# An attention and gated MLP block on one core: denominators' reciprocals spread by two DMAs through HBM in place of a VectorE transposition, with a changed planner

## The chip, the cores and the metric

The kernel runs on one core of one Trainium2 chip. Its time is the device time in microseconds (us); lower is better. Before the change it takes 1222.69 us, the median of 3 runs (1222.42 to 1225.06).

The engines are TensorE (PE, with its weight loads shown as PEld), VectorE (DVE), ScalarE (ACT), GpSimd (POOL) and SyncE (SP). Each runs its own list of instructions in a fixed order and waits on semaphores of the others. The core's 16 DMA engines move data; an engine's queue issues the transfers (SPq is SyncE's).

## What is computed

All inputs and the output are bf16. In short (`x` is 2048 x 512, 32 heads, 2048 cached keys and values a head, 128 wide; the MLP is 1792 wide):

```python
xn = _layernorm(x)
q = (xn @ wq).reshape(B, Sq, H, Dh)            # per head: 2048 x 128
p = softmax(q @ k_cache.T * Dh ** -0.5)        # per head: 2048 x 2048
s = (p @ v_cache).reshape(Sq, H * Dh) @ wo
r = relu(xn @ w1 + b1)
g = silu((r * r) @ w2 + b2)
out = x + s * g
```

## The kernel before

**Blocks, heads and pairs.** The 2048 rows are cut into NQB = 4 blocks of QB = 512. A block runs through 32 heads, so there are NG = 128 units, called heads below and numbered g. A head's 2048 keys are 16 tiles of 128, taken two at a time: NPR = 8 steps a head, NPAIR = 1024 steps in all (loop at L1421).

**One step.** `gen_scores` (L670) multiplies two key tiles with the queries into PSUM (psA), transposed, so that keys lie on partitions; ScalarE takes the exponential of 128 x 1024 values into one of NPT = 8 buffers pT. Two steps later `gen_pv` (L964) multiplies by V. Between them come one or two matmuls of filler work from a list of jobs: the query projection of later heads (`job_proj`), the MLP (`job_h`, `job_o2`) and the output projection (`job_wo`).

**Two kinds of heads.** In the first kind pT is stationary and V, widened by a column of ones, streams: 64 matmuls of 129 columns a head. The denominator falls out as the 129th column, one value a row on its own partition; VectorE copies the sum out (o_un), takes the reciprocal, GpSimd scales, and a transposing DMA turns the result into oT. In the second kind (V stationary, `gen_pv_b`, L725) 16 matmuls of 512 columns give the output already transposed; ScalarE copies it to o_col (NOC = 3 buffers). The denominator must then be summed over keys, which lie on partitions, and be spread over all 128 partitions along the row. Heads 0 to 2 and the last 3 are of the first kind; for the others `choose` (called at L1425) takes the second kind when VectorE's debt `owed` (L960) is under OWED = 9000 ns. m counts the heads of the second kind; buffers of the denominators' chain alternate by m % 2.

**The denominators' chain before.** For each pT buffer either VectorE sums it alone in one transposing reduction (`den_part`, L744), or GpSimd first adds its halves (`part_add`, L757, into h_sum) and VectorE reduces 512 columns (`part_half`, L765). `den_sum` (L776) adds the eight steps to d_sum, 128 x 16, in which every group of 32 partitions holds a partial sum. `den_write` and `den_read` (L783, L790) are two DMAs on SyncE: to d_scr in HBM, and back with all four groups on every partition. `den_total` (L798) adds the four, `den_recip` (L804) inverts, and `den_spread` (L809) is a transposition on VectorE of 32 x 32 blocks of a broadcast, which writes r_all, 128 x 512 f32, one buffer. `den_scale` (L817) on GpSimd multiplies o_col by r_all into oT.

**What sets the order.** The program emits every engine's list ahead of time with a model of each engine's clock (`_cost`; `_ISSUE` at L97 gives a DMA's issue and landing times). Small VectorE work waits in the list `quiet` with a due step and is placed by `fill_dve` (L904) where VectorE has room; `fill_pool` (L921) and `fill_sync` (L948) do the same for GpSimd and SyncE as soon as the model says that an operand is there. `ready_at` (L890) adds SLACK = 1500 ns to what depends on a DMA (den_total, den_read). `fill_pool` takes a `part_add` whenever GpSimd is free and one of three h_sum buffers is. On the chip the order is fixed; a wait stops what stands behind it.

**Loads.** SyncE also issues all keys (two transposing DMAs a head, `fill_k`, L628), values (four a head, `fill_v`, L640) and query weights, two to three heads ahead, and between steps 2 and 150 the MLP's and output weights.

**LayerNorm.** Each block's four tiles of 128 rows are loaded to x_ln (`ln_load`, L474), normalised (`ln_bn`, `ln_rstd`, `ln_scale`) to xn_t and transposed by DMA (`ln_next`, L517). x_ln and xn_t have four tiles each.

Helper lines in the profile: L226 and L231 matmuls (the second for the first kind of heads and the first head), L235 activations, L239 tensor-tensor, L245 and L249 tensor-scalar forms, L253 copies, L257 reciprocals, L282 reductions, L286 transposing reductions, L290 the transposition, L294 DMAs, L298 transposing DMAs.

Of the kernel before, what the change touches and what calls it, by code (L numbers as in the profile page):

```python
# [84 lines left out]
def _uses_port(name, fn):  # L85
# [3 lines left out]
    if name == "DVE":  # L89
        if f in (_tt, _stt):  # L90
            return _in_sbuf(k["in0"]) and _in_sbuf(k["in1"])
        if f in (_ts, _copy):
# [6 lines left out]
          "d_quad": (1230, 4200)}  # L99
# [201 lines left out]
def bass_recurrent_scan__mha_block_cached__dense_activation_squared_relu__prompt_kernel(  # L301
# [41 lines left out]
    OWED = 9000  # L343
# [16 lines left out]
    NSL, NSW, NQS, NPT, NOT, NOC, NHS = 3, 4, 3, 8, 3 * HC, 3, 3  # L360
# [20 lines left out]
    d_sum = sb("d_sum", [P, 2, NBK], F32)  # L381
    d_quad = sb("d_quad", [P, 2, 4, NBK], F32)
    d_rec = sb("d_rec", [P, 2, NBK], F32)
    r_all = sb("r_all", [P, NBK, 32], F32)
    d_scr = nc.dram_tensor("d_scr", [2, 32, 4 * NBK], F32, kind="Internal").ap()
# [6 lines left out]
    x_ln = sb("x_ln", [P, TPB, D], BF16)  # L392
    xn_t = sb("xn_t", [P, TPB, D], BF16)
    st_t = sb("st_t", [P, TPB, 12], F32)
    mv_t = sb("mv_t", [P, TPB, 2], F32)
    nm_t = sb("nm_t", [P, TPB], F32)
# [3 lines left out]
    warm = sb("warm", [P, P], BF16)  # L400
# [33 lines left out]
    sl_dr = [S.slot(f"dr{i}") for i in range(2)]  # L434

# [22 lines left out]
    t_ones = None  # L458
    for i in range(NSL):
        t_ones = E(GP, partial(_memset, out=v_sb[:, i, :, Dh:Dh + 1], val=1.0))  # L460
# [12 lines left out]

    def ln_load(j, i, eng=SP):  # L474
        jt = j * TPB + i
        t_xl[jt] = S.emit_dma(
            eng, partial(_dma, out=x_ln[:, i, :], in_=A_x[0, jt * P:(jt + 1) * P, :]), sl_xl[i],
            deps=[t_xn.get(jt - TPB)])
# [3 lines left out]
    def ln_bn(j, i, c0=0, c1=D):  # L482
        jt = j * TPB + i
        k = 6 if c0 else 0
        t_bn[jt] = E(DV, partial(_bn_stats, out=st_t[:, i, k:k + 6], in_=x_ln[:, i, c0:c1]),
                     deps=[t_xl[jt], t_xn.get(jt - TPB), t_xr.get(jt - TPB)])
# [15 lines left out]
    def ln_scale(j, i):  # L502
        jt = j * TPB + i
        t_xn[jt] = E(DV, partial(_ts, out=xn_t[:, i, :], in0=x_ln[:, i, :],
                                 scalar1=mv_t[:, i, 0:1], scalar2=rstd[:, i:i + 1],
                                 op0=ALU.subtract, op1=ALU.mult),
                     deps=[t_xr[jt], t_xnr.get(jt - TPB)])

    def ln_transpose(j, i):
        jt = j * TPB + i  # L510
        t_xnr[jt] = tok_xT[j][i] = S.emit_dma(
            SP, partial(_dmaT, out=xnT[:, :, jt % (2 * TPB) * P:(jt % (2 * TPB) + 1) * P],
                        in_=xn_t[:, i, :]),
            sl_xT[i], deps=[t_xn[jt], t_xuse.get(j - 2)])
        assert j < 2 or n_xuse[j - 2] == NFC + H

    def ln_next(j, i):  # L517
        ln_scale(j, i)
        ln_transpose(j, i)

# [38 lines left out]
    def first_transpose(i):  # L559
        for c in range(NDC):  # L560
            t_xT[i] = E(PE, partial(_peT, out=bankF(1)[:, 0:256].bitcast(BF16)[:, c * P:(c + 1) * P],
                                    in_=xn_t[:, i, c * P:(c + 1) * P], ident=ident[:]),
                        deps=[t_xn[i], t_ident, tok_xT[0][i - 1] if i else None],
                        inc=(c == NDC - 1))
        t_xnr[i] = t_xT[i]
# [147 lines left out]
    t_sum = {}  # L713
    t_dw = {}
    t_dr = {}
# [60 lines left out]
    def den_sum(g):  # L776
        m = b_no[g]
        t_sum[m] = E(DV, partial(_reduce, out=d_sum[:, m % 2, :],
                                 in_=d_part[:, m % 2, 0:len(t_parts[g]), :].rearrange(
                                     "p n b -> p b n")),  # L780
                     deps=t_parts[g] + [t_dw[m - 2] if m >= 2 else None])

    def den_write(g):  # L783
        m = b_no[g]
        dst = bass.AP(tensor=d_scr.tensor, offset=d_scr.offset + m % 2 * P * NBK,
                      ap=[[NBK, 4], [4 * NBK, 32], [1, NBK]])
        t_dw[m] = S.emit_dma(SP, partial(_dma, out=dst, in_=d_sum[:, m % 2, :]), sl_dw[m % 2],
                             deps=[t_sum[m], t_dr[m - 2] if m >= 2 else None])

    def den_read(g):  # L790
        m = b_no[g]
        src = bass.AP(tensor=d_scr.tensor, offset=d_scr.offset + m % 2 * P * NBK,
                      ap=[[0, 4], [4 * NBK, 32], [1, 4 * NBK]])
        t_dr[m] = S.emit_dma(SP, partial(_dma, out=d_quad[:, m % 2].rearrange("p a b -> p (a b)"),
                                         in_=src), sl_dr[m % 2],
                             deps=[t_dw[m], t_tot[m - 2] if m >= 2 else None])

    def den_total(g):  # L798
        m = b_no[g]
        t_tot[m] = E(DV, partial(_reduce, out=d_rec[:, m % 2, :],  # L800
                                 in_=d_quad[:, m % 2].rearrange("p a b -> p b a")),
                     deps=[t_dr[m], t_spr.get(m - 2)])

    def den_recip(g):  # L804
        m = b_no[g]
        t_rec[m] = E(DV, partial(_recip, out=d_rec[:, m % 2, :], in_=d_rec[:, m % 2, :]),
                     deps=[t_tot[m]])

    def den_spread(g):  # L809
        m = b_no[g]  # L810
        base = d_rec[:, m % 2, :]
        spread = bass.AP(tensor=base.tensor, offset=base.offset,
                         ap=[list(base.ap[0]), [1, NBK], [0, 32]])
        t_spr[m] = E(DV, partial(_transpose32, out=r_all[:], in_=spread),
                     deps=[t_rec[m], t_scale[m - 1] if m else None])

    def den_scale(g):  # L817
        m = b_no[g]
        t_scale[m] = tok_oT[g] = E(
            GP, partial(_tt, out=oT[:, g % NOT, :], in0=o_col[:, m % NOC, :],  # L820
                        in1=r_all[:].rearrange("p b i -> p (b i)"), op=ALU.mult),
            deps=[t_col[m], t_spr[m], t_wodone[g - NOT] if g >= NOT else None])
# [5 lines left out]
    tiles = {}  # L828
    WEIGHT = {den_part: 1130, part_half: 610, den_sum: 350, den_total: 170, den_recip: 130,
              den_spread: 600}  # L830
# [4 lines left out]
    def plan_b(g):  # L835
        tiles[g] = 0
        first = NPR * g
        for k in range(NPR):
            calm(first + k + NPT - 2, partial(den_part, NPR * g + k))
        calm(first + NPR + 6, partial(den_sum, g))  # L840
        sync_quiet.append(partial(den_write, g))
        sync_quiet.append(partial(den_read, g))
        calm(first + NPR + 12, partial(den_total, g))
        calm(first + NPR + 12, partial(den_recip, g))
        calm(first + NPR + 13, partial(den_spread, g))
        pool_quiet.append(partial(den_scale, g))

    def needs(fn):
# [6 lines left out]
        if f in (den_sum, den_total, den_recip, den_spread, den_scale, den_write, den_read):  # L855
            g = a[0]
            m = b_no[g]
            if f is den_sum:
                if tiles[g] < NPR:
                    return None  # L860
                return t_parts[g] + [t_dw.get(m - 2) if m >= 2 else t_parts[g][0]]
            if f is den_write:
                return [t_sum.get(m), t_dr.get(m - 2) if m >= 2 else t_sum.get(m)]
            if f is den_read:
                return [t_dw.get(m), t_tot.get(m - 2) if m >= 2 else t_dw.get(m)]
            if f is den_total:
                return [t_dr.get(m), t_spr.get(m - 2) if m >= 2 else t_dr.get(m)]
            if f is den_recip:
                return [t_tot.get(m)]
            if f is den_spread:  # L870
                return [t_rec.get(m), t_scale.get(m - 1) if m else t_rec.get(m)]
            return [t_col.get(m), t_spr.get(m)]
# [17 lines left out]
    def ready_at(fn):  # L890
        toks = needs(fn)
        if toks is None or any(t is None for t in toks):
            return None
        slack = SLACK if fn.func in (den_total, den_read) else 0
        return S.ready(toks) + slack
# [25 lines left out]
    def fill_pool(until):  # L921
        while GP.t < until:
# [6 lines left out]
            if x < NHS or t_half[x - NHS] is not None:  # L929
# [127 lines left out]
    def at(step, fn):  # L1057
        events.setdefault(step, []).append(fn)
# [141 lines left out]
    def load_xt(jt):  # L1200
        if jt < NQB * TPB:
            tok_xt[jt] = S.emit_dma(
                GP, partial(_dma, out=x_t[:, jt % 2, :], in_=A_x[0, jt * P:(jt + 1) * P, :]),
                sl_xt[jt % 2], deps=[t_u[jt - 2] if jt >= 2 else None])
# [142 lines left out]
    for j in range(NQB):  # L1347
        if j + 1 < NQB:
            for i in range(TPB):
                at(j * SPB + 3 * NPR, partial(ln_load, j + 1, i))  # L1350
# [59 lines left out]
    t_bankF[:] = [t_q0[3], tok_xT[0][3]]  # L1410
    gen_pv(3)
# [9 lines left out]
    for pi in range(NPAIR):  # L1421
        g, k = divmod(pi, NPR)
        if k == 0 and g > 0:
            m = len(b_heads)
            choose(g, FIRST_B <= g < NG - 3 and owed(pi) < OWED and (m < NOC or m - NOC in t_dr))  # L1425
            if is_b(g):
                plan_b(g)
# [78 lines left out]
```

## Time and profile before

| | before |
|---|---|
| median of 3 runs | 1222.69 us |
| profiled execution | 1225.06 us, span 1223.3 us |
| granted TensorE clock | 1.00 |
| PE busy | 1207.6 us (99% of the span) |
| DVE, ACT, POOL busy | 1083.0, 1090.1, 1074.9 us (89, 89, 88%) |
| DMA | 174.80 MB, 143 GB/s; SyncE's queue 69.0% of the 16 engines' span |
| heads with V stationary | 113 (count of o_col and of r_all) |
| r_all on VectorE (L290) | 113 x 680 ns, 76.8 us |
| oT on GpSimd (L239) | 113 x 1274 ns, 143.9 us |
| h_sum on GpSimd (L239) | 772 x 1166 ns, 876.3 us |
| d_part from h_sum, from pT (L286) | 772 x 685 ns, 132 x 1210 ns |

The profile is of one execution. Busy times are sums of an engine's instructions without the waits; matmuls are pipelined, so two that follow each other overlap in the rows, and the distance between their starts is the time each one costs. A few matmul records are missing from a trace. An idle engine costs nothing unless TensorE, or what TensorE waits for, stands behind it.

### The profile page before, as it was taken

Reading aid. Unit: us, or ns where it says so; the run is one execution under the profiler, and the core shown is the slowest. Engines: PE = TensorE matmul, PEld = TensorE weight load, DVE = VectorE, ACT = ScalarE, POOL = GpSimd, SP = SyncE. Lnnn points to the kernel's source line nnn. Section 1 sums busy time; section 2 is a strip of 40 time slices with the busy share of each in tenths; the row PEclk is TensorE's granted clock in tenths of the full one; section 3 lists DMA queues with packets and bytes.
Section 4 is the critical chain, followed back from the end, with each engine's and each line's share of the span. In section 5 each row is a group of like instructions: output and inputs, shape, how many; then the busy total and the mean of one; then the engine's idle time right before and its main releaser. Section 6 shows DMA issues by size and latency. Waiting matters only on the chain.

```text
span 1223.3 us, 19712 instructions
## 1 busy us (share of the span) xinstructions
PE 1207.6 (99%) x6339; PEld 585.9 (48%) x6461; DVE 1083.0 (89%) x1829; ACT 1090.1 (89%) x1158; POOL 1074.9 (88%) x986
## 2 busy tenths in 40 slices
PE   9999999999999999999999999999999999999998
PEld 7544444444545444444544445444445454444555
DVE  4689989999998999989899998889999999999973
ACT  7888999999898999999998998999999989989995
POOL 1788999999897999999888998999998979999881
PEclk9999999999999999999999999999999999999999
DMA  9998978667777666666777666667667666667661
GB/s 199 190 210 170 188 158 157 133 132 137 143 152 148 133 135 134 135 136 127 149 143 159 133 135 146 133 131 141 132 138 149 138 143 138 131 129 134 130 137 32
DMA packets 665567, 174.80 MB, mean 143 GB/s; under 512 B 652248, under 2 KB 664280, under 8 KB 665464
## 3 DMA queue, kind: packets, MB, share of 16 engines
q1 hardware_dynamic: 663368, 169.47, 69.0%
q0 software_dynamic: 1424, 3.81, 1.2%
q8 instruction: 51, 0.84, 0.3%
q14 instruction: 52, 0.43, 0.1%
q10 hardware_dynamic: 672, 0.26, 0.1%
HBM read 100.31 MB, written 3.02 MB: 84 GB/s over the span
## 4 chain that ended last, share of the span: by engine, by line
PE 92%; DVE 3%; POOL 2%; issue 1%; DMA 1%; ACT 0%; ACTq 0%; SPq 0%; POOLq 0%
PE psA L226 34%; PE psO L226 30%; PE psF L226 24%; PE psO L231 4%; POOL h_sum L239 1%; DVE d_part L286 1%; DMA d_quad<-d_scr 0%; ACT pT L235 0%; DVE h2T L249 0%; POOL oT L239 0%; DVE acc L249 0%; DVE r_t L245 0%; PE psA L231 0%; DMA d_scr<-d_sum 0%; DMA x_ln<-in_A_x_dram 0%
## 5 line engine op out<-in xcount | busy, mean ns | idle before, releaser
L235 ACT ACTIVATE pT<-psA 128x1024 bf16<-128x1024 f32 x1025 | 1037.7, 1025 | 114.0 <-PE psA L226 74.2
L239 POOL TENSOR_TENSOR h_sum<-pT 128x512 f32<-128x512 bf16 x772 | 876.3, 1166 | 43.6 <-DVE d_part L286 23.5
L226 PE MATMUL psA<-qt_sb,kT 128*128 128x512 bf16 x1972 | 591.5, 379 | 5.0 <-ACT pT L235 2.3
L286 DVE TRANSPOSE_TENSOR_REDUCE d_part<-h_sum 128x16 f32<-128x512 f32 x772 | 512.7, 685 | 32.5 <-POOL h_sum L239 29.7
L226 PE MATMUL psO<-pT,v_sb 128*128 128x512 bf16 x1771 | 529.7, 379 | 2.6 <-DVE o_un L253 0.5
L226 PEld LDWEIGHTS psA<-qt_sb,kT 128*128 128x128 bf16 x2032 | 193.6, 98 | 216.4 <-ACT pT L235 5.5
L226 PEld LDWEIGHTS psO<-pT,v_sb 128*128 128x128 bf16 x1808 | 176.7, 98 | 213.9 <-issue 2.3
L226 PE MATMUL psF<-xnT,wq_sb 128*128 128x512 bf16 (+1 forms) x510 | 165.9, 374 | 2.4 <-DVE h2T L249 1.2
L239 POOL TENSOR_TENSOR oT<-o_col,r_all 128x512 bf16<-128x512 f32 x113 | 143.9, 1274 | 23.1 <-DVE r_all L290 22.4
L286 DVE TRANSPOSE_TENSOR_REDUCE d_part<-pT 128x32 f32<-128x1024 bf16 x132 | 158.9, 1210 | 3.5 <-ACT pT L235 3.3
L226 PE MATMUL psF<-wo_all,oT 128*128 128x512 bf16 x471 | 161.2, 379 | 0.7
L253 DVE CAST qt_sb<-psF 128x512 bf16<-128x512 f32 (+1 forms) x130 | 86.6, 666 | 24.6 <-PE psF L226 22.5
L226 PEld LDWEIGHTS psF<-xnT,wq_sb 128*128 128x128 bf16 x520 | 50.2, 98 | 62.4 <-issue 3.1
L290 DVE STREAM_TRANSPOSE r_all<-d_rec 128x512 f32<-128x512 f32 x113 | 76.8, 680 | 0.4
L226 PE MATMUL psF<-xnT,w_sb 128*128 128x512 bf16 x221 | 76.2, 379 | 0.5 <-DVE h2T L249 0.2
L231 PEld LDWEIGHTS psO<-v_sb,pT 128*128 128x128 bf16 x960 | 63.8, 98 | 26.8 <-ACT pT L235 0.4
L226 PEld LDWEIGHTS psF<-wo_all,oT 128*128 128x128 bf16 x480 | 46.9, 98 | 56.4
L231 PE MATMUL psO<-v_sb,pT 128*128 128x129 bf16 x960 | 73.7, 220 | 0.1
L226 PE MATMUL psF<-w_sb,h2T 128*128 128x512 bf16 x221 | 72.7, 379 | 0.4
L235 ACT ACTIVATE o_col<-psO 128x512 f32<-128x512 f32 x113 | 66.8, 591 | 0.0
L245 DVE TENSOR_SCALAR r_t<-psF,b1f 128x512 bf16<-128x512 f32 x56 | 41.2, 736 | 12.3 <-PE psF L226 11.0
L282 DVE TENSOR_REDUCE d_sum<-d_part 128x16 f32<-128x144 f32 (+3 forms) x113 | 43.2, 382 | 1.0
(61 smaller groups left out, 407.4 us busy)
## 6 DMA issues: line engine op xcount, KB each, us to landing
v_sb<-in_A_v_cache_dram SPq DMA_DIRECT2D x508, 128.0 KB, 2.6
wq_sb<-in_A_wq_dram SPq DMA_DIRECT2D x127, 128.0 KB, 2.7
wo_all<-in_A_wo_dram SPq DMA_DIRECT2D x16, 256.0 KB, 3.1
kT<-in_A_k_cache_dram SPq DMA_TRANSPOSE x254, 3.4
d_quad<-d_scr SPq DMA_DIRECT2D x113, 32.0 KB
w_sb<-in_B_w_dram SPq DMA_DIRECT2D x14, 256.0 KB, 3.6
x_t<-in_A_x_dram POOLq DMA_DIRECT2D x16, 128.0 KB, 3.0
x_ln<-in_A_x_dram SPq DMA_DIRECT2D x15, 128.0 KB, 2.7
```

The source lines that it names most:

```text
L226: return e.matmul(out, lhsT, rhs, start=start, stop=stop)
L231: return e.matmul(out, lhsT, rhs, start=start, stop=stop, skip_group_check=True)
L235: return e.activation(out, in_, func, bias=bias, scale=scale)
L239: return e.tensor_tensor(out, in0, in1, op)
L245: return e.tensor_scalar(out, in0, scalar1=scalar1, scalar2=scalar2, op0=op0, op1=op1)
L253: return e.tensor_copy(out, in_)
L282: return e.tensor_reduce(out, in_, axis=AX.X, op=ALU.add)
L286: return e.tensor_reduce(out, in_, axis=AX.X, op=ALU.add, apply_transpose=True)
L290: return e.transpose(out, in_)
```

## The change

- The reciprocals are no longer spread by VectorE. `den_turn`, a VectorE transposition of 128 x 32, puts d_sum's blocks into rows before the write, `den_read` brings the four partial sums to 32 partitions only, `den_total` and `den_recip` work on these 32, and two new DMAs on SyncE, `rec_write` and `rec_read`, write the 512 reciprocals to r_scr in HBM and read them back onto all 128 partitions. r_all has two buffers; o_col has four (NOC = 4).
- The planner: OWED is 8000; GpSimd takes a part_add only while VectorE's debt is over POOL_OWED = 3500; SLACK also stands before rec_read and den_scale; part_half gets HALF_SLACK = 600.
- Space: x_ln and xn_t have two tiles each; block 0's tiles 2 and 3 use x_t and out_t, later blocks load tiles 2 and 3 after tiles 0 and 1 are scaled. The warm-up operand lies in o_bf.
- The change's title names 116 heads with V stationary. The number and size of the load pieces (NKP, NVP, NWP) are the same in both kernels.

The diff, cut to its core:

```diff
-          "d_quad": (1230, 4200)}
+          "d_quad": (530, 4200), "r_scr": (530, 2200), "r_all": (1230, 4400)}
...
-    OWED = 9000
+    OWED = 8000
+    POOL_OWED = 3500
+    HALF_SLACK = 600
...
-    NSL, NSW, NQS, NPT, NOT, NOC, NHS = 3, 4, 3, 8, 3 * HC, 3, 3
+    NSL, NSW, NQS, NPT, NOT, NOC, NHS = 3, 4, 3, 8, 3 * HC, 4, 3
...
-    r_all = sb("r_all", [P, NBK, 32], F32)
-    d_scr = nc.dram_tensor("d_scr", [2, 32, 4 * NBK], F32, kind="Internal").ap()
+    r_all = sb("r_all", [P, 2, QB], F32)
+    d_scr = nc.dram_tensor("d_scr", [2, P, 32], F32, kind="Internal").ap()
+    r_scr = nc.dram_tensor("r_scr", [2, QB], F32, kind="Internal").ap()
...
+    t_sum0 = E(GP, partial(_memset, out=d_sum[:], val=0.0))
...
     def ln_next(j, i):
         ln_scale(j, i)
         ln_transpose(j, i)
+        if i + 2 < TPB:
+            ln_load(j, i + 2)
...
+    def den_turn(g):
+        m = b_no[g]
+        t_row[m] = E(DV, partial(_transpose32, out=d_row[:, m % 2, :], in_=d_sum[:, m % 2, :]),
+                     deps=[t_sum[m], t_dw.get(m - 2)])
...
-        dst = bass.AP(tensor=d_scr.tensor, offset=d_scr.offset + m % 2 * P * NBK,
-                      ap=[[NBK, 4], [4 * NBK, 32], [1, NBK]])
-        t_dw[m] = S.emit_dma(SP, partial(_dma, out=dst, in_=d_sum[:, m % 2, :]), sl_dw[m % 2],
-                             deps=[t_sum[m], t_dr[m - 2] if m >= 2 else None])
+        t_dw[m] = S.emit_dma(SP, partial(_dma, out=d_scr[m % 2], in_=d_row[:, m % 2, :]),
+                             sl_dw[m % 2], deps=[t_row[m], t_dr.get(m - 2)])
...
-                      ap=[[0, 4], [4 * NBK, 32], [1, 4 * NBK]])
+        src = bass.AP(tensor=d_scr.tensor, offset=d_scr.offset + m % 2 * P * 32,
+                      ap=[[NBK, 32], [32 * 32, 4], [1, NBK]])
+        t_dr[m] = S.emit_dma(SP, partial(_dma, out=d_quad[0:32, m % 2], in_=src), sl_dr[m % 2],
+                             deps=[t_dw[m], t_tot.get(m - 2)])
...
-    def den_spread(g):
+    def rec_write(g):
         m = b_no[g]
-        base = d_rec[:, m % 2, :]
-        spread = bass.AP(tensor=base.tensor, offset=base.offset,
-                         ap=[list(base.ap[0]), [1, NBK], [0, 32]])
-        t_spr[m] = E(DV, partial(_transpose32, out=r_all[:], in_=spread),
-                     deps=[t_rec[m], t_scale[m - 1] if m else None])
+        t_rw[m] = S.emit_dma(
+            SP, partial(_dma, out=r_scr[m % 2].rearrange("(p b) -> p b", b=NBK),
+                        in_=d_rec[0:32, m % 2, :]),
+            sl_rw[m % 2], deps=[t_rec[m], t_spr.get(m - 2)])
+
+    def rec_read(g):
+        m = b_no[g]
+        src = bass.AP(tensor=r_scr.tensor, offset=r_scr.offset + m % 2 * QB,
+                      ap=[[0, P], [1, QB]])
+        t_spr[m] = S.emit_dma(SP, partial(_dma, out=r_all[:, m % 2, :], in_=src), sl_rr[m % 2],
+                              deps=[t_rw[m], t_scale.get(m - 2)])
...
-        slack = SLACK if fn.func in (den_total, den_read) else 0
+        slack = SLACK if fn.func in (den_total, den_read, rec_read, den_scale) else (
+            HALF_SLACK if fn.func is part_half else 0)
...
-            if x < NHS or t_half[x - NHS] is not None:
+            if (x < NHS or t_half[x - NHS] is not None) and owed(now[0]) > POOL_OWED:
...
-                at(j * SPB + 3 * NPR, partial(ln_load, j + 1, i))
+                if i < 2:
+                    at(j * SPB + 3 * NPR, partial(ln_load, j + 1, i))
```

## The prediction

> **What bounds the kernel now.** I read the page's busy line first, then the busy time by stretches, then the chain of waits, then the timeline around the places where TensorE stood still. The busy line and four stretches (columns: start:end, length, then busy time of PE, PEld, DVE, ACT, POOL with the instruction counts, the granted clock, the DMA engines' share, GB/s):
>
> ```profile
> PE 1207.6 (99%) x6339; PEld 585.9 (48%) x6461; DVE 1083.0 (89%) x1829; ACT 1090.1 (89%) x1158; POOL 1074.9 (88%) x986
> ```
> ```profile
> 50.00:110.00 60.00, 55.24 (x295) 26.23 (x300) 53.64 (x91) 48.92 (x53) 49.80 (x48) 1.00 0.91 189
> 110.00:300.00 190.00, 189.05 (x864) 86.12 (x881) 172.77 (x294) 173.55 (x186) 185.26 (x167) 1.00 0.76 154
> 300.00:320.00 20.00, 19.35 (x137) 10.64 (x137) 18.79 (x31) 16.75 (x18) 17.18 (x17) 1.00 0.86 144
> 320.00:660.00 340.00, 338.21 (x1685) 160.10 (x1718) 312.23 (x527) 309.13 (x328) 310.45 (x283) 1.00 0.69 140
> ```
>
> TensorE is the bound, at full granted clock, and it is nearly gapless. From 110 to 300 us it lacks 0.95 of 190 us (0.5%), from 320 to 660 us 1.79 of 340 us (0.5%); the same 0.5% everywhere is what some missing matmul records would leave, so I count it as no idle time. Above that 0.5% only two places are left: 50 to 110 us, 60 - 55.24 = 4.8 us less 0.3, so 4.4 us; and 300 to 320 us, 0.65 less 0.1, so 0.5 us. The first 50 us lack 1.6 us in the start-up, which the change leaves as it is. So **at most 4.9 us can be won from idle time**, almost all of it in one early stage.
>
> What that stage waits for (timeline: start, length, engine, what it does, then the idle time before it and who ended it):
>
> ```profile
> 54.72 3.04 SPq L298 DMA_TRANSPOSE kT<-in_A_k_cache_dram  x1
> 57.81 0.69 SPq L294 DMA_DIRECT2D d_scr<-d_sum  x1
> 58.55 0.98 SPq L294 DMA_DIRECT2D v_sb<-in_A_v_cache_dram  x2
> 60.77 0.57 SPq L294 DMA_DIRECT2D d_quad<-d_scr  x1
> ```
> ```profile
> 63.14 0.26 DVE L282 TENSOR_REDUCE d_rec<-d_quad 128x16 f32<-128x64 f32 x1 [3.91 <-DMA d_quad<-d_scr]
> ```
> ```profile
> 64.16 1.15 POOL L239 TENSOR_TENSOR h_sum<-pT 128x512 f32<-128x512 bf16 x1 [4.58 <-DVE d_rec L257]
> ```
> ```profile
> 100.88 3.65 DVE L245 TENSOR_SCALAR xn_t<-x_ln,mv_t,rstd 128x512 bf16<-128x512 bf16 x1
> ```
>
> SyncE's queue is late (a transposing load took 3.04 us to issue), the denominators' round trip through HBM lands late, VectorE stands 3.91 us in its fixed order, GpSimd 4.58 us behind it, and TensorE pays when the next evacuations come late. At 100.88 us a scaling that takes 0.37 us at its quickest takes 3.65 us beside GpSimd's adds. The list of waits agrees: ACT's own waits are 74 us for TensorE's scores, and 5.2 us for h_sum.
>
> **The change, part by part.**
>
> *Fewer heads of the old kind.* o_col is written 113 times, so 15 of 128 heads have P stationary; with the 116 that the change's title names, 12 do. Late in the trace eight 129-column matmuls of such a head start at 1206.42 and the next scores at 1206.87: 0.45 us. Two 512-column matmuls start at 1205.99 and the next begins at 1206.42: 0.43 us. The difference, 0.02 us, occurs 8 times a head: 3 x 8 x 0.02 = **-0.5 us** of TensorE work.
>
> *VectorE.* The spread goes: 113 x 0.68 us = 77 us. A transpose of 32 columns comes in its place. No row has that size; the nearest are the cast of 14 columns (0.164) and the reduction 128x64 (0.228), I take 0.17 us, so 116 x 0.17 = 20 us. den_total and the reciprocal work on 32 partitions instead of 128 with equal lengths: 0.228 and 0.236 us stay. Three more heads, each 8 halves x 0.685 + 0.38 + 0.23 + 0.24 + 0.17 = 6.5 us, less two o_un copies (0.42 each) and a reciprocal (0.17), cost 5.5 x 3 = 16 us. Sum: -77 + 20 + 16 = -41 us of 1083 us. None of it is on TensorE's path outside the two idle places. In 50 to 110 us some five heads pass the den steps: 5 x 0.51 = 2.6 us of relief. HALF_SLACK of 0.6 us acts against the 29.7 us in which VectorE waited for h_sum (75 times, mean 0.4 us).
>
> *GpSimd.* POOL_OWED lets it take a half only while VectorE owes 3.5 us. A direct part costs VectorE 1.21 us instead of 0.685 and spares GpSimd 1.17 us; if all 41 us went that way, 41 / 0.525 = 78 parts, and GpSimd would lose 91 of 1075 us. In 110 to 300 us it is busy 185.26 of 190 us, so a margin there is worth something: it is what absorbs the waits below. In return den_scale now waits for a DMA instead of a VectorE instruction, and behind it in GpSimd's order stand h_sum adds, then the parts, then the pT buffers that ACT writes.
>
> *Two more DMAs a head on SyncE.* The reciprocals' write lands like d_scr's: 2.94 us in the chain of waits (to 60.75). The read fills 128 x 2 KB = 256 KB; the row of that size is wo_all, 3.1 us to landing, and 128 KB loads land in 2.6 to 2.7. Beside the 0.68 that goes, the chain grows by 2.9 + 3.1 + 0.2 - 0.7 = 5.5 us, and by up to 3 us of planned slack (SLACK twice). From o_col to the scaled head it takes 17.1 us now (median in the trace, 26.6 at most); o_col gets a fourth buffer, 4 x 9.3 us = 37 us instead of 28 at the 9.3 us a head takes, so this buffer does not become the wait. The Trainium skill, DMA: Bandwidth & Descriptors, Latency and other measured facts, speaks against the change where traffic is dense: HBM access goes from 0.2 us on average to 2 us at high load. By it, at the share of 0.91, the two hops would be an estimated 4 us longer; d_scr's 2.94 us at 57.81 against a shortest 1.96 us between its issue and d_quad's is the row that leans that way, by only 1 us a hop.
>
> Issue time: d_scr and d_quad take 0.56 to 0.57 us each, so 1.1 us a head more. Between 320 us and the end of the loads, SyncE issues or waits for some 68% of the time; with 1.1 of 9.3 us more it is 80%. The trace shows 80% in 110 to 200 us already, where TensorE lost nothing, so later stages should carry it. The two new issues also wait in SyncE's fixed order, one for the reciprocal, one for the write's landing, and behind them stand V, K and query-weight loads that the scores and products of later heads wait for. Between 50 and 100 us SyncE is at 83 to 100%; head 7's last V piece landed 2.2 us before its first exponential, and head 8's 4.4, later ones 6 or more. Only head 3's extra DMAs precede head 7's loads: 1.1 us of 2.2. So the loads themselves stay hidden; without that cover each further us would be paid.
>
> *DMA engines.* 116 x 256 KB = 30 MB more on 175 MB. By bytes that would take the mean share in later stages from 0.68 to 0.80; as 2 KB pieces instead of the under-512-byte packets that make up 652,248 of 665,567, less. 110 to 200 us ran at 0.88 without a loss; I take nothing.
>
> *LayerNorm tiles.* Two loads move from step 24 to after the scaling of tiles 0 and 1, two tiles borrow x_t and out_t: 2 x 0.5 us of issue leave the crowded stretch; the scaling itself (0.37 to 3.65 us) stays. Zero, bounds -0.5 to +1 (another scaling beside an add). The memset of d_sum stands beside the start-up's (0.1 to 0.2 us on GpSimd, before V's ones): zero, at most 0.2.
>
> *The end.* The last V-stationary head is read by the output projection at 1209.16; now it is scaled by 1197.65. The longer chain (5.5 to 8.5 us) moves this to 1203 to 1206: hidden, with 3 us to spare.
>
> **The sum**, on the profiled execution (1225.06, span 1223.3): -0.5 for the heads; of the 4.9 us of idle time I take half, -2.5, because VectorE's relief is 2.6 us in that stage and because the late d_quad, which starts the trouble, is not removed. That gives 1222.1. Bounds: -4.9 if all goes, +6 if the new waits win (third rival). The median of the runs is 1222.69, 2.4 below the profiled execution. The one place where executions can differ much is that early stage, so the median run probably holds about 2.5 us of it; half is 1.2, and 1222.69 - 0.5 - 1.2 = **1221.0**.
>
> **The rivals.**
> - *All early idle time goes.* For: five of its causes (DVE chain, GpSimd's adds, the waits for h_sum) are eased. Against: d_quad is as late as before. 1222.69 - 0.5 - 2.5 = 1219.7, and 1217.3 if the median run held the whole 4.9.
> - *The freed time is only handed over.* Direct parts refill VectorE, GpSimd idles instead, TensorE's gaps stay: 1222.69 - 0.5 = 1222.2.
> - *Slower: GpSimd waits for r_all.* The place is 57 to 200 us, with 15 V-stationary heads, where SyncE is 80 to 100% taken and in fixed order. If the landing is behind the plan as d_quad was (3.9 us), den_scale holds the adds. GpSimd has 190 - 185.26 = 4.7 us in 110 to 300 us and what POOL_OWED gives. At 1 us a head it decides for slower: 15 - 4.7 = 10 us of lag, of which eight pT buffers hide about half, so +5: 1227.
>
> **How the numbers follow.** A measurement of this kernel can tell about 0.2% (2.4 us) from no change. Forecast 0.35 (0.06 of it faster, 0.29 within); all idle time goes 0.25, faster; handed over 0.10, within; GpSimd waits 0.30, slower. So faster 0.31, within 0.39, slower 0.30. The range 1218.3 to 1228: below, the middle of the second case; above, the third with 1 us to spare; for the likeliest case alone 1219.5 to 1222.7.
>
> **What would show it.** Right: the stretch 50 to 110 us shows PE above 57 us busy, all later ones keep their 0.5%, d_rec to r_all a chain of two landings of 2 to 3 us, and waits for r_all short. Wrong: GpSimd's oT waits for the DMA of r_all in many heads with ACT waiting for h_sum; PE below 99.4% after 110 us; a stop before psA or psF in the last 15 us for the last V-stationary head; or 80% of SyncE turning into late kT or v_sb.

## The result and the profile after

The changed kernel takes 1218.97 us, the median of 6 runs (1217.59 to 1221.24), beside 1222.75 for the kernel before on the same chip (6 runs): a ratio of 0.9967, 95% interval 0.9954 to 0.998. That is faster by 3.8 us (0.3%), inside the range 1218.3 to 1228 with 0.7 us to spare, but 2 us below the likeliest case (1221.0) and nearest to the case "all early idle time goes" (1219.7). The profiled execution took 1218.81 us, span 1217.0.

The busy line of the page and the same four stretches, of the changed kernel:

```profile
PE 1206.0 (99%) x6197; PEld 579.2 (48%) x6317; DVE 1063.5 (87%) x1856; ACT 1089.7 (90%) x1161; POOL 1060.5 (87%) x971
```
```profile
50.00:110.00 60.00, 59.03 (x316) 28.63 (x322) 53.00 (x97) 52.73 (x57) 50.45 (x48) 1.00 1.02 206
110.00:300.00 190.00, 188.95 (x863) 85.75 (x879) 168.88 (x295) 172.72 (x186) 180.06 (x163) 1.00 0.92 181
300.00:320.00 20.00, 19.84 (x138) 11.06 (x140) 18.36 (x31) 17.64 (x19) 15.49 (x15) 1.00 0.89 173
320.00:660.00 340.00, 338.23 (x1685) 159.83 (x1717) 304.83 (x529) 309.32 (x330) 303.07 (x276) 1.00 0.84 163
```

TensorE is the second number behind each window. From 50 to 110 us it is busy 59.03 instead of 55.24 us, from 300 to 320 us 19.84 instead of 19.35; elsewhere the 0.5% is unchanged. These 4.3 us are most of the 6.3 us by which the span fell. Three heads of the old kind make 0.5 us more, and the first head begins 0.4 us sooner. The rest, about 1 us, could not be placed, since a gap as long as one matmul looks like a missing record. The profiled execution of before was 2.3 us above its median, so 4.3 us is more than a median run gained there.

Where the denominators' trip begins, SyncE and VectorE in the timeline of the changed kernel (start, length, engine, operation):

```profile
54.16 0.50 SPq L294 DMA_DIRECT2D d_scr<-d_row  x1
...
56.00 1.64 SPq L298 DMA_TRANSPOSE kT<-in_A_k_cache_dram  x1
57.69 0.57 SPq L294 DMA_DIRECT2D v_sb<-in_A_v_cache_dram  x1
58.31 0.50 SPq L294 DMA_DIRECT2D d_quad<-d_scr  x1
```
```profile
63.28 0.20 DVE L282 TENSOR_REDUCE d_rec<-d_quad 32x16 f32<-32x64 f32 x1
```

d_scr is issued at 54.16 instead of 57.81 us and d_quad at 58.31 instead of 60.77; VectorE no longer stands still in front of d_rec (no bracket at the end of the line). That has two reasons: d_quad comes sooner, and VectorE's order reaches d_rec only at 63.28 us, where before it stood there from 59.23 us on. That SyncE's queue was late before, and not the sum, is seen in VectorE's timeline of the kernel before:

```profile
50.35 0.37 DVE L282 TENSOR_REDUCE d_sum<-d_part 128x16 f32<-128x128 f32 x1
```

The sum was ready at 50.72 us, and d_scr was issued 7.1 us later; in the changed kernel (d_row ready at 51.67 us) it is 2.5 us. The new DMA, from the view by tile of r_all and the list of waits:

```profile
L294 SPq DMA_DIRECT2D r_all<-r_scr x116: 325/503/1605, 72.3 to 1193.4; - x116
L239 POOL TENSOR_TENSOR oT<-o_col,r_all x116: 1257/1269/1731, 77.2 to 1196.8; 128x512 bf16<-128x512 f32 x116
its engine sat idle before it (us, times) until:
  DMA r_all<-r_scr: 21.4, 10
...
DMA to landing us min/median/max: 3.1/4.0/5.6
```
```profile
POOL oT L239 <- DMA r_all<-r_scr: 21.4, 10, 6.3
...
ACT pT L235 <- POOL h_sum L239: 3.6, 8, 1.0
```

GpSimd now waits 21.4 us for r_all to land, in 10 heads; before, it waited 22.4 us, 16 times, for VectorE's transposition. ACT's waits for h_sum fell from 5.2 to 3.6 us. The longer chain did not make a new stop.

### The profile page after: what moved, and what is told of

Same layout as the page of the kernel before. It is cut to its first block, busy times and chain, and to the rows that moved or that the text cites. A ratio compares the mean times of both kernels' runs of the same rounds, so it can differ in the third digit from the quotient of the medians.

```text
span 1217.0 us, 19731 instructions
## 1 busy us (share of the span) xinstructions
PE 1206.0 (99%) x6197; PEld 579.2 (48%) x6317; DVE 1063.5 (87%) x1856; ACT 1089.7 (90%) x1161; POOL 1060.5 (87%) x971
## 4 chain that ended last, share of the span: by engine, by line
PE 95%; DVE 1%; issue 1%; POOL 1%; DMA 1%; ACT 1%; SPq 0%; ACTq 0%; POOLq 0%
PE psA L226 36%; PE psO L226 32%; PE psF L226 25%; PE psO L231 3%; DMA d_quad<-d_scr 1%; POOL h_sum L239 1%; ACT pT L235 1%; DVE d_part L286 0%; PE psA L231 0%; SPq L298 0%; SPq L294 0%; POOL oT L239 0%; DVE z_t L239 0%; PE psF L270 0%; DVE st_t L274 0%
## 5 line engine op out<-in xcount | busy, mean ns | idle before, releaser
L239 POOL TENSOR_TENSOR h_sum<-pT 128x512 f32<-128x512 bf16 x756 | 861.0, 1167 | 63.4 <-ACT pT L235 34.8
L226 PE MATMUL psO<-pT,v_sb 128*128 128x512 bf16 x1816 | 543.9, 380 | 1.8
L286 DVE TRANSPOSE_TENSOR_REDUCE d_part<-h_sum 128x16 f32<-128x512 f32 x756 | 495.7, 680 | 26.1 <-POOL h_sum L239 25.1
L226 PEld LDWEIGHTS psO<-pT,v_sb 128*128 128x128 bf16 x1856 | 181.4, 98 | 219.1 <-issue 0.6
L286 DVE TRANSPOSE_TENSOR_REDUCE d_part<-pT 128x32 f32<-128x1024 bf16 x172 | 208.1, 1214 | 8.2 <-ACT pT L235 7.5
L239 POOL TENSOR_TENSOR oT<-o_col,r_all 128x512 bf16<-128x512 f32 x116 | 148.2, 1278 | 21.5 <-DMA r_all<-r_scr 21.4
L231 PEld LDWEIGHTS psO<-v_sb,pT 128*128 128x128 bf16 x768 | 50.9, 98 | 21.1 <-ACT pT L235 0.4
L231 PE MATMUL psO<-v_sb,pT 128*128 128x129 bf16 x768 | 59.0, 221 | 0.1
L282 DVE TENSOR_REDUCE d_sum<-d_part 128x16 f32<-128x160 f32 (+4 forms) x116 | 45.9, 396 | 1.8
L249 DVE SCALAR_TENSOR_TENSOR h2T<-psF,b1f,r_t 128x512 bf16<-128x512 f32 x56 | 41.9, 747 | 1.7
```

Of the source, the lines that this page charges most:

```text
L226: return e.matmul(out, lhsT, rhs, start=start, stop=stop)
L231: return e.matmul(out, lhsT, rhs, start=start, stop=stop, skip_group_check=True)
L239: return e.tensor_tensor(out, in0, in1, op)
L249: return e.scalar_tensor_tensor(out=out, in0=in0, scalar=scalar, in1=in1, op0=op0, op1=op1)
L282: return e.tensor_reduce(out, in_, axis=AX.X, op=ALU.add)
L286: return e.tensor_reduce(out, in_, axis=AX.X, op=ALU.add, apply_transpose=True)
```

## The experiments

Theory A is the prediction's: the spread relieves VectorE, and that fills the early gaps. The other theories are named in the expectations. Each kernel has its own runs of the kernel before beside it; ratios are against those, with a 95% interval in brackets. The changed kernel was not run again beside the experiments, so a difference against its 1218.97 us is one between two sets of runs (the kernel before has 1222.62 to 1222.83 in them, 1222.75 beside the change). The intervals of experiments 2, 3, 4, 6, 7, 10 and 12 overlap with that of the change; those of 5, 8, 9 and 11 lie above it, and that of 1 touches it.

**1. Only the LayerNorm tiles.** The kernel before, with x_ln and xn_t of two tiles and the later loads of tiles 2 and 3; its core:

```diff
-    x_ln = sb("x_ln", [P, TPB, D], BF16)
-    xn_t = sb("xn_t", [P, TPB, D], BF16)
+    x_ln = sb("x_ln", [P, 2, D], BF16)
+    xn_t = sb("xn_t", [P, 2, D], BF16)
...
+        if i + 2 < TPB:
+            ln_load(j, i + 2)
...
-                at(j * SPB + 3 * NPR, partial(ln_load, j + 1, i))
+                if i < 2:
+                    at(j * SPB + 3 * NPR, partial(ln_load, j + 1, i))
```

> The kernel before with only the LayerNorm part of the change: x_ln and xn_t of two tiles, block 0's tiles 2 and 3 in x_t and out_t, later tiles 2 and 3 loaded after the scaling of tiles 0 and 1. 113 heads with V stationary, the old spread, the old planner constants. Theory A (VectorE's relief by the spread fills the early gaps): no gain, 1222.7 within 1 us, 50 to 110 us still lacks some 4 us of TensorE. Rival B (SyncE's queue was too full before 60 us, and the two loads that leave it put the denominators' DMAs on time): most of the gain, 1219 to 1220. Rival C (the planner's reserves): no gain, 1222.7.

Measured: 1221.09 us (before 1222.62), ratio 0.9989 (0.998 to 0.9998). Its stretch and SyncE's timeline:

```profile
50.00:110.00 60.00, 58.36 (x313) 28.41 (x318) 56.66 (x95) 52.36 (x56) 53.87 (x52) 1.00 0.86 191
```
```profile
52.09 0.68 SPq L294 DMA_DIRECT2D d_scr<-d_sum  x1
52.82 0.98 SPq L294 DMA_DIRECT2D v_sb<-in_A_v_cache_dram  x2
54.74 0.56 SPq L294 DMA_DIRECT2D d_quad<-d_scr  x1
```

The chain's first DMAs are issued 6 us sooner than before (d_quad 54.74 against 60.77; d_scr follows its sum after 1.8 us instead of 7.1), and 3.1 of the 4.4 us of early idle time are gone in the profiled execution, without the spread. Theory A falls for that part. Not all of the 6 us is the two loads': SyncE reaches the two loads that stay at 40.07 us here and at 43.09 before. Counted from there, d_quad comes 3.0 us sooner (14.67 us after them instead of 17.68). By the median it is 1.5 us, not the 3 of rival B; the gap at 300 to 320 us stays (19.26 of 20 us busy).

**2. Everything but the spread.** The first experiment plus the planner's constants of the change:

```diff
-    OWED = 9000
+    OWED = 8000
+    POOL_OWED = 3500
+    HALF_SLACK = 600
```

o_col keeps its three buffers here, so its fourth is left out together with the spread.

> The changed kernel without its spread: LayerNorm tiles and the planner's constants of the change (OWED 8000, POOL_OWED 3500, HALF_SLACK 600) on the old spread by VectorE. The planner then finds 107 heads with V stationary. Theory A: the early gaps stay in part and six more heads of the other kind than before cost 6 x 0.16 = 1 us: 1222.5 to 1224. Rival B: 1220. Rival C: the early idle time goes, -3, +1 for the heads: 1220 to 1221.

Measured: 1220.34 us, 0.998 (0.9972 to 0.9989), with TensorE busy 19.84 of 20 us in 300 to 320, and early:

```profile
50.00:110.00 60.00, 59.63 (x320) 29.16 (x325) 56.88 (x96) 53.86 (x57) 50.59 (x48) 1.00 0.96 202
```

So without the spread the early gaps are gone altogether, although the planner takes 107 heads. What the spread with its buffers adds is 1220.34 - 1218.97 = 1.4 us, though the intervals overlap, and it brings nine heads more. At the 0.16 us a head of experiment 7 these are 1.4 us: no other gain of the spread shows. Whether the nine heads come from VectorE's relief or from the fourth buffer was not tested.

**3. The spread without two of the constants.**

```diff
-    POOL_OWED = 3500
-    HALF_SLACK = 600
+    POOL_OWED = -1
+    HALF_SLACK = 0
```

> The changed kernel with POOL_OWED and HALF_SLACK taken out (GpSimd adds whenever it is free, halves without reserve), OWED 8000: 116 heads with V stationary as in the change. Theory A: as fast as the change, 1218 to 1220, early gaps gone. Rival C: the gaps are back, 1221 to 1223, with GpSimd above 97% busy in 110 to 300 us and ACT waiting for h_sum as long as before (5 us) or longer. Rival B: 1219.

Measured: 1220.38 us, 0.9985 (0.9977 to 0.9994); ACT waits 7.0 us for h_sum. The early stretch is full (59.69 of 60 us), but other gaps open: 300 to 320 us has 18.96 us busy, 900 to 1180 us 277.11 of 280 against 278.60. That profiled execution took 1222.34 us, 2 us above the median, so its gaps are larger than a median run's. Part of rival C holds: the constants keep 1.4 us by the medians. Its GpSimd share above 97% in 110 to 300 us did not come (178.16 of 190).

**4. More heads with V stationary.** OWED = 10000, 119 heads.

> The changed kernel with OWED 10000 instead of 8000: 119 heads with V stationary, three of the other kind fewer. If a head of the old kind costs 0.16 us more on TensorE, as the distances between matmuls say, 1218.5; if it costs 0.4 us in all, 1217.8; if VectorE's debt of up to 10 us brings the gaps back, 1220 to 1222.

Measured: 1220.11 us, 0.9981 (0.9972 to 0.999). At 0.16 us a head the three heads would be worth 0.5 us, yet it is not faster than the change. The early stretch is full (59.68 of 60 us); 300 to 320 us has 19.41 us busy against 19.84, and 900 to 1180 us 277.97 against 278.60. That VectorE's larger debt opens these gaps, as the last case said, is not shown, and since the intervals overlap the size stays open too.

**5. Only the two loads late.** The kernel before with one line changed:

```diff
-                at(j * SPB + 3 * NPR, partial(ln_load, j + 1, i))
+                at(j * SPB + (3 * NPR if i < 2 else 8 * NPR + 4 * NPR * (i - 2) + 12),
+                   partial(ln_load, j + 1, i))
```

> The kernel before with one edit: the loads of LayerNorm tiles 2 and 3 of the next block are issued at steps 76 and 108 of a block instead of step 24; tiles, buffers, spread and constants are as before, 113 heads with V stationary. Theory D (what the tiles alone brought in the first experiment, -1.5 us, is that SyncE's queue loses two issues ahead of the first denominators): 1221.1 within 0.7, the first d_quad issued 3 to 6 us earlier than at 60.8 us, TensorE busy above 58 us in 50 to 110 us. Rival E (it is the place of the tiles or chance): 1222.6, d_quad near 60.

Measured: 1221.69 us (before 1222.83), 0.9994 (0.9985 to 1.0003): by time unclear. The trace has what theory D expects, d_quad at 55.38 us and the stretch full to 58.71 us:

```profile
50.00:110.00 60.00, 58.71 (x319) 28.44 (x318) 56.61 (x96) 52.31 (x56) 53.85 (x52) 1.00 0.89 191
110.00:300.00 190.00, 190.00 (x882) 86.14 (x881) 172.95 (x295) 173.40 (x187) 185.05 (x168) 1.00 0.76 154
```

The second line also shows that the even 0.5% was missing records: here TensorE is busy 190.00 of 190 us.

Up to the two loads that stay at step 24, SyncE's list is the same in both kernels, and still it is not there at the same time. First the kernel before, then this one:

```profile
43.09 0.98 SPq L294 DMA_DIRECT2D x_ln<-in_A_x_dram  x2
```
```profile
40.82 0.98 SPq L294 DMA_DIRECT2D x_ln<-in_A_x_dram  x2
...
52.79 0.68 SPq L294 DMA_DIRECT2D d_scr<-d_sum  x1
...
55.38 0.56 SPq L294 DMA_DIRECT2D d_quad<-d_scr  x1
```

So 2.3 of the 5.4 us by which d_quad is earlier stood ahead of the edit: a difference between the executions, of which the profiled one of before is the slowest of its six. The other 3.1 us come behind the place of the loads. The stage itself is sure. From the start of ScalarE's exponential of step 40 to that of step 80 the execution of before takes 52.53 us (56.36 to 108.89) and this one 48.51 (56.20 to 104.71); from there to the last one they take 1099.1 and 1099.4 us. In these two executions the whole difference is 4.0 us of this stage; by the medians it is 1.1 us.

**6. Two loads put back into the changed kernel.** Two 128 KB loads at step 24, into a buffer that nothing reads at that time:

```diff
+    for i in range(2):
+        at(24, partial(load_more, i))
```

> The changed kernel with two more loads of 128 KB at step 24 on SyncE, into out_t, which nothing reads: the queue is again as full there as in the kernel before. Theory D: the early gap is back in part, +1 to +2 us on the change, 1220 to 1221. If the planner's reserves and the spread carry the early stage too, no difference, 1219.

Measured: 1220.62 us, 0.9983 (0.9974 to 0.9992), so 1.65 us above the change. That is the size theory D gave, though the intervals overlap. d_quad is issued at 58.81 us, hardly later than 58.31, and VectorE does not wait for it, as in the change; but SyncE had reached the loads at step 24 1.0 us sooner than in the change (40.36 against 41.40 us), so from there on it loses 1.5 us to d_quad. It falls back further: the second r_all is issued at 83.77 us instead of 82.53. GpSimd's next oT in the changed kernel, then in this one, with ScalarE behind it:

```profile
88.18 1.27 POOL L239 TENSOR_TENSOR oT<-o_col,r_all 128x512 bf16<-128x512 f32 x1 [1.63 <-DMA r_all<-r_scr]
```
```profile
89.38 1.26 POOL L239 TENSOR_TENSOR oT<-o_col,r_all 128x512 bf16<-128x512 f32 x1 [2.25 <-DMA r_all<-r_scr]
91.84 3.05 ACT L235 ACTIVATE pT<-psA 128x1024 bf16<-128x1024 f32 x3 [0.81 <-POOL h_sum L239]
```

GpSimd is 1.2 us late at r_all, ScalarE waits 0.81 us for the h_sum behind it, and TensorE for ScalarE. From the exponential of step 40 to that of step 80 the changed kernel takes 47.71 us (55.97 to 103.68) and this one 48.70 (56.12 to 104.82); from there to the last one both take 1098.4 us. So in the profiled executions the two loads cost 1.0 us, all of it in the early stage, by a full queue and a late r_all: the route of the prediction's slower rival, on a small scale. The sign agrees in experiments 1, 5 and 6, at 1.1 to 1.7 us by the medians; only experiment 1 is clear of the noise by itself, and then barely.

**7. Ten more old heads.** `choose` gets `and not (40 <= g < 112 and g % 6 == 0)`.

> The changed kernel with every sixth head from 42 to 108 forced to P stationary, 106 heads with V stationary instead of 116, all in the stretch without idle time. By the distances between matmuls, 0.16 us a head: +1.6 us, 1220.6. If a head of the old kind costs nothing because the relief of VectorE and GpSimd pays for it, 1219; if it costs 0.4 us with what follows, 1223.

Measured: 1220.53 us, 0.9983 (0.9974 to 0.9992): 1220.53 - 1218.97 = 1.56 us for ten heads, **0.16 us a head**, what the distances between matmuls said. The intervals overlap, but the traces agree with the medians: from the exponential that opens head 42 to the one that opens head 111, the changed kernel takes 643.55 us (404.15 to 1047.70) and this one 645.24 (403.98 to 1049.22), 1.7 us for the ten heads; ahead of that stretch both take 395.83 us, and behind it 154.33 and 154.34.

**8. No reserve in front of the new waits.**

```diff
-        slack = SLACK if fn.func in (den_total, den_read, rec_read, den_scale) else (
+        slack = SLACK if fn.func in (den_total, den_read) else (
```

> The changed kernel without SLACK ahead of rec_read and den_scale; 116 heads with V stationary. Tests the slower rival's mechanism: GpSimd placed 1.5 us earlier at the landing of r_all. If a wait for r_all on GpSimd reaches TensorE: POOL oT waits for r_all of 60 us or more instead of 21, ACT waits for h_sum of 8 us or more instead of 3.6, TensorE idle 3 us more, 1221 to 1224. If GpSimd's order has room, waits as long but 1219.

Measured: 1223.2 us, 1.0008 (0.9999 to 1.0017): 4.2 us slower than the change, and no faster than the kernel before. The waits for r_all grew, less than expected, and ACT's for h_sum did not (3.7 us). The list of waits, then the last stretch, then VectorE's timeline ahead of a gap of TensorE at 921 us:

```profile
POOL oT L239 <- DMA r_all<-r_scr: 36.5, 22, 9.3
```
```profile
900.00:1180.00 280.00, 278.25 (x1336) 127.73 (x1335) 258.02 (x440) 254.50 (x273) 259.40 (x231) 1.00 0.83 161
```
```profile
914.37 3.46 DVE L249 SCALAR_TENSOR_TENSOR acc<-acc,g_all 128x512 f32<-128x512 f32 x1
917.76 0.68 DVE L253 CAST qt_sb<-psF 128x512 bf16<-128x512 f32 x1
918.36 1.88 DVE L286 TRANSPOSE_TENSOR_REDUCE d_part<-h_sum 128x16 f32<-128x512 f32 x3
920.17 0.70 DVE L245 TENSOR_SCALAR r_t<-psF,b1f 128x512 bf16<-128x512 f32 x1
```

This gap does not follow a wait for r_all. It follows a gating that took 3.46 us (0.65 at its quickest), while GpSimd ran three h_sum adds from 913.90 to 917.28 us, and then the evacuations queued behind it. So the reserve is worth 4 us, but this gap did not come by the route of the slower rival. Taking the reserve out moves the whole order, and with it what falls beside what; that this is how most of the 4 us are lost is argued, not shown.

**9 and 10. The constants one by one.** HALF_SLACK = 0, and POOL_OWED = -1, each in the changed kernel.

> The changed kernel with HALF_SLACK 0 (POOL_OWED stays): 116 heads with V stationary. If the reserve before the halves is what keeps TensorE fed: VectorE waits for h_sum 45 us or more instead of 25, TensorE idle +3 us, 1221 to 1222. If POOL_OWED does it: 1219.

> The changed kernel without POOL_OWED (HALF_SLACK stays): 115 heads with V stationary, +0.16 us for the one head. If leaving GpSimd idle while VectorE owes little is what keeps TensorE fed: ACT waits for h_sum 6 us or more instead of 3.6, TensorE idle +2 us, 1221. If HALF_SLACK does it: 1219.2.

Measured: 1220.53 us, 0.9991 (0.9982 to 0.9999), without HALF_SLACK; 1219.02 us, 0.9973 (0.9963 to 0.9983), without POOL_OWED. Of the two it is HALF_SLACK, the reserve in front of the halves. The list of waits and the stretches that suffer, of experiment 9 (an execution of 1222.69 us, 2.2 above its median):

```profile
DVE d_part L286 <- POOL h_sum L239: 45.4, 120, 1.1
```
```profile
300.00:320.00 20.00, 18.53 (x114) 9.36 (x115) 19.23 (x32) 16.17 (x18) 16.71 (x17) 1.00 0.77 156
320.00:660.00 340.00, 337.35 (x1651) 158.17 (x1683) 306.90 (x534) 308.08 (x327) 309.55 (x281) 1.00 0.82 165
```

VectorE stands 120 times for an add of GpSimd (45.4 us) instead of 56 times (25.1 us), and TensorE loses 1.3 us in 300 to 320 us against the change and 0.9 in 320 to 660.

**11. More reserve.** SLACK = 2000; the planner then takes 117 heads.

> The changed kernel with SLACK 2000 instead of 1500 at every landing of the chain: 117 heads with V stationary. As the reserve without which 4 us were lost, more of it should shorten the waits for r_all (21 us) and d_quad (4.4 us): 1218.0 to 1218.8, TensorE idle 0.5 us less, one head 0.16 less. If 1.5 us already covers the landings, or the longer chain holds o_col, 1219 to 1220.

Measured: 1221.62 us, 0.9994 (0.9985 to 1.0003). The expectation fails: the waits for r_all fell only to 18.8 us, those for d_quad rose to 9.7, and gaps opened elsewhere (187.36 of 190 us busy in 110 to 300).

**12. The other two loads late as well.** SLACK 1800, and

```diff
-                    at(j * SPB + 3 * NPR, partial(ln_load, j + 1, i))
+                    at(j * SPB + 6 * NPR + 8 * i, partial(ln_load, j + 1, i))
```

> The changed kernel with SLACK 1800 and the two LayerNorm loads that are still at step 24 issued at steps 48 and 56: 116 heads with V stationary. By theory D (fewer issues on SyncE ahead of the first denominators) the gap that is left in 50 to 110 us (about 1 us) goes and d_quad is issued before 57 us: 1218.0. If what is left there comes from GpSimd, 1219.

Measured: 1219.7 us, 0.999 (0.9979 to 1.0002), single runs from 1218.58 to 1225.76. The early gap is gone in its profiled execution (59.68 of 60 us), as theory D has it, but d_quad was issued at 57.25 us, hardly sooner, and that execution (1225.76 us) loses some 5.4 us between 110 and 320 us beyond the missing records (granted clock 0.99 from 110 to 300, where the others have 1.00). Its five slowest runs, 1223.46 us and more, show a mean clock of 0.999, the other seven 1.000. Two edits at once; not settled. No kernel here is clearly faster than the change.

## Why the prediction was right, and which terms were not

The range held the time, at its lower end; it was 10 us wide and spanned four cases, and the time lies below the 1219.5 to 1222.7 of the likeliest one. Faster by more than 0.2% had been given 0.31, no clear change 0.39. So that the range held is in part owed to its width. The bound was right: TensorE, at full clock, with 4.9 us to win. What failed is who wins them.

- **Heads, -0.5 us.** Right: 0.16 us a head, by experiment 7 and its trace.
- **Half of the early idle time, because of VectorE's relief of 2.6 us.** Both the size and the cause were off. In the profiled executions 4.3 of 4.9 us went. Without the spread, experiment 1 loses 3.1 of them and experiment 2 all.
- **LayerNorm tiles, "zero, bounds -0.5 to +1".** This is the step that failed: measured -1.5 us (experiment 1), and -1.1 by the two loads alone (experiment 5, not clear of the noise). I had counted the two loads' issue time on a crowded queue (1.0 us), but not that this queue was what the first denominators waited for. The late d_quad was in the prediction's own lines, as the start of the trouble.
- **"The late d_quad is not removed."** Wrong in part for that reason: 58.31 us instead of 60.77, and VectorE, which also comes to it 4 us later in its order, did not wait for it.
- **HALF_SLACK** got one sentence and no term; experiment 9 puts it at 1.6 us.
- **VectorE, -41 us of busy time.** Measured 1083.0 to 1063.5, -19.5. The planner turned part of it into direct parts: 172 instead of 132. The transposition of 32 columns takes 0.19 us on average (0.17 taken). GpSimd fell by 14 us, not the 91 at most. "The freed time is only handed over" holds for about half of it.
- **The chain.** r_all lands in 4.0 us at the median, not 3.1; from o_col to the scaled head it takes 26.9 us at the median in the trace, 9.8 us more, where 5.5 to 8.5 were expected, and 38.1 at most: just over the 37 us that four buffers were to cover, without a stop that shows: each buffer was free 3.2 us or more before its next writing.
- **DMA and SyncE.** The share in 320 to 660 us rose to 0.84; by bytes I had 0.80 as the upper end. From 50 to 110 us it reads 1.02. SyncE's queue went to 77 to 79% after 200 us (80% expected). None of it shows on TensorE after 110 us. By the Trainium skill, DMA: Bandwidth & Descriptors, Latency and other measured facts (HBM access of 2 us at high load), the two new hops had been estimated 4 us longer. The trace gives half of that: r_all's median of 4.0 us is 0.9 above its quickest of 3.1, and r_scr's of 2.4 is 1.1 above its 1.3.
- **The slower rival** did not come with the reserve of 1.5 us in place. Its route exists: in experiment 6 it costs 1.0 us. Experiment 8 reaches its time (1223.2), but the gap followed there came another way.
- **The end.** The last V-stationary head is scaled at 1198.0 us, TensorE's first long run of output projections starts at 1202.94: hidden, as predicted.

## What to carry to other kernels

When a static order stands still at one late DMA, ask first what else its queue issues ahead of it: moving two loads that were not yet needed was worth 1.1 to 1.5 us by the medians, about as much as nine heads of the change's own aim. The relief of an engine that was 89% busy but off the bound was worth only what it let the planner choose differently (0.16 us a head), while a planned reserve in front of an in-order wait (0.6 us before each half, 1.5 us before each landing of the new DMAs) was worth 1.6 and 4 us; with 2.0 us instead of 1.5 at every landing the time was 2.65 us worse. And a profile is one execution: before two traces are compared, see how far each lies from its median.

## What the runs showed that was not expected

VectorE's gatings stretch beside GpSimd's instructions: the groups of the 16 gatings, of the changed kernel and of experiment 9 (busy us, mean ns behind the bar):

```profile
L249 DVE SCALAR_TENSOR_TENSOR acc<-acc,g_all 128x512 f32<-128x512 f32 x16 | 25.9, 1621 | 0.1
```
```profile
L249 DVE SCALAR_TENSOR_TENSOR acc<-acc,g_all 128x512 f32<-128x512 f32 x16 | 30.1, 1882 | 0.0
```

The quickest takes 0.64 us, the mean is 1.6 to 1.9, and the longest, in experiments 3, 8 and 9, took 4.4 us. Of the 80 gatings of the kernel before, the changed kernel and these three, the ten that no GpSimd instruction overlapped took 0.64 to 0.68 us. Some beside an add were as quick, but each one above 1.2 us ran beside h_sum adds, and the 4.4 us spans several GpSimd instructions in a row. Of the late gaps that I followed, three (experiment 8 at 613 and 921 us, experiment 9 at 312 us) lie within 8 us behind such a gating; a fourth, experiment 9 at 923 us, does not. In the changed kernel four gatings took over 2.5 us and no gap of TensorE followed, so a long one alone is not enough. Small edits of the planner moved the time by 1 to 4 us; that the place of these instructions does it is likely, not shown. It is the scatter against which every experiment here has to be read.
